# Four-token query loads with DMA transposes, bank-seeded first-layer sums and a third seven-product tile in a fused attention and MoE kernel

## The chip, the cores and the metric

One Trainium2 chip, one of its cores. Time is device microseconds (us) of one execution; the kernel before took 347.33 us, the median of three runs (346.93 to 353.17). The profile is one further execution: 350.85 us, of which 349.2 us are the span from its first to its last instruction and 1.65 us lie around it. Predicted and measured times are medians of such runs.

The engines are TensorE (PE, with its weight loads as PEld), VectorE (DVE), ScalarE (ACT), GpSimd (POOL) and SyncE (SP). Each runs its own instructions in the order of the program and waits on semaphores for the others. SP and POOL issue most DMAs; an instruction that waits on such a queue holds up everything behind it.

## What is computed

```python
B, H, S, D = 8, 8, 576, 64                       # attention, band of +-32 tokens
scores = q @ k.T / sqrt(D); masked where |i - j| > 32
attn = softmax(scores);  a = attn @ v
x = a as (4608 tokens, 512)
h = x @ w_in                                     # (512, 2048)
g = h * sigmoid(1.702 * h)
out = g @ w_out                                  # (2048, 512), float32
```

The 8 batches of 576 tokens are one row of N = 4608 tokens. A query needs only keys of its own batch that lie at most 32 tokens away.

## The kernel before

**Units and tiles.** A unit is 128 queries, shifted by 32 against the keys: unit u holds queries 128u+32 to 128u+159, as two blocks of 64, and each block meets two sets of 64 keys. Four units make a tile of 512 tokens; there are 36 units and 9 tiles. The output of a unit goes to rows 128u+32 and up.

**Attention of a unit.** `scores` runs 32 matmuls of 64 by 64 (weights are keys from `kT`, the moving operand queries from `qT`) and one exponential on ACT. `band` (DVE) multiplies with the mask. `values` runs 16 matmuls, with V from `ve` for the even block and from `vo` for the odd one; `vo` is V shifted by 64 tokens, two copies made by `odd_v`. `norm` (DVE) makes the reciprocal of the sums and writes `x` (float16, two buffers). `x_T` transposes `x` to `xT`, on PE in the head, by a DMA transpose from SP later.

**Loads of q and k.** All loads that change type are issued by POOL. `load_heads` puts four neighbouring tokens of all heads on a partition (a run of 1 KB in memory); PE transposes these (`heads_T`), and `put_T` writes them to `kT` or `qT`, with the token order restored. `load_units` puts one token on a partition (runs of 256 bytes), in one DMA for each 128 tokens, two where a batch ends inside; `units_X` then issues four DMA transposes for a tile. `kT` is a ring of 1536 tokens and `qT` one of 1024, each with a copied piece past its end (`wrap`). Before the change tiles 0 to 2 come by `load_heads` (tile 3 for keys), the rest by `load_units`. The staging tiles `ks` and `qs` have two buffers each, so a load waits until the transposes of two tiles earlier have read theirs.

**First and second layer.** In plain form a half tile (256 tokens) takes 64 matmuls of 256 columns in the first layer (`layer1`), a unit 16 matmuls of 512 columns in the second (`layer2`). A tile can instead go by seven products of quarter matrices (Winograd's form of Strassen's method): 112 matmuls of 256 columns in each layer, with sums of the operands made beforehand (`w_in_sums`, `x_sums`; `g_sums`, `w_out_sums`) and sums of the products made behind. `first_layer` has four groups; a group has seven products, named 1, 2, 6, 7, 5, 4, 3 in that order. Its two banks are A (products 1, 6, 5, 3) and E (2, 7, 4). Products 1 and 2 add up to c11: ACT copies the first one from its bank to SBUF, DVE adds the other one (L429), and ACT forms g from it. Products 6 and 7 are copied out (L442 on ACT, L446 on DVE), 5 and 4 added on DVE (L450, L454), 3 read by ACT. Each bank is filled again by the next product, so a product waits for the evacuation of the one before it in its bank. `second_layer` has 28 calls of four matmuls, on banks o and t; its last product goes out by a DVE copy (L512).

**Order.** `head` does the attention of units 0 to 6, the first layer of half tiles 0 to 2 and the second layer of units 0 to 3, all plain; `pairs` goes on in plain form; then come steps T = 3 to 10. A step does the attention of tile T, the first layer of tile T-1 and the second layer of tile T-2, in the order of the string `STEP`: S, M and V with a digit are scores, mask and values (with `norm` and `x_T`) of one of the four units; a digit and a digit is group and product of `first_layer`; c is the next call of the second layer; G, g.., o are operand sums; L issues the loads of q and k of tile T+3, l those of V; X issues the transposes of tile T+2; x has POOL make the x sums of tile T and the `vo` copies. Before the change, tiles 0 to 2 are plain and tiles 3 to 8 go by seven products; `first_layer` starts with T = 4 and `second_layer` with T = 5; d in STEP is a plain first-layer call, in T = 3 only.

Of the kernel before, what the change touches and what calls it, by code (L numbers as in the profile page):

```python
# [9 lines left out]
def _safe_warn_once(msg, *a, **kw):  # L10
# [15 lines left out]
QRING = 1024  # L26
NO = 5
STEP = ("L S0 S1 M0 M1 G c 01 c c c S2 M2 c 02 S3 M3 T d c V0 l 06 c V1 d c 07 c V2 05 c V3 X o "
        "04 c 11 c 03 d 22 c x 12 21 c 16 17 c 26 d 15 c g00 27 14 d c 25 13 c 24 c d 23 g11 c 32 c d 31 d w c c 36 37 c 35 g22 c 34 c 33 c c c")


class _Kernel:
# [50 lines left out]
    def setup(self):  # L83
# [7 lines left out]
        self.kT = cst.tile([128, 4, RING + 64], BF16, name="kT")  # L91
        self.qT = cst.tile([128, 4, QRING + 32], BF16, name="qT")
        self.k_first = cst.tile([128, 4, 64], BF16, name="k_first")
        self.q_first = cst.tile([128, 4, 32], BF16, name="q_first")
# [41 lines left out]
    def pieces(self, lo, n):  # L136

        at = lo
        while at < lo + n:
            b, s = divmod(at, self.S)  # L140
            m = min(self.S - s, lo + n - at)
            yield at - lo, b, s, m
            at += m

    def load_heads(self, i, c, heads=None):
# [6 lines left out]
        for off, b, s, m in self.pieces(512 * i, 512):  # L152
            self.nc.gpsimd.dma_start(self.stage[key][off // JT:(off + m) // JT, lo:hi, :],
                                     src[b, lo:hi, s:s + m, :].rearrange("h (p j) d -> p h (j d)", j=JT))

    def load_units(self, c, i):


        st = self.stage[c, i] = self.work.tile([128, 4, self.H, self.D], BF16, name=c + "s", tag=c + "s", bufs=2)
        src = {"q": self.q, "k": self.k}[c]  # L160
        for u in range(4):
            for off, b, s, n in self.pieces(512 * i + 128 * u, 128):
                self.nc.gpsimd.dma_start(st[off:off + n, u], src[b, :, s:s + n, :].rearrange("h s d -> s h d"))  # L163

    def units_X(self, c, i):
        dst, ring = {"q": (self.qT, QRING), "k": (self.kT, RING)}[c]
        at = (512 * i) % ring
        for u in range(4):
            self.nc.sync.dma_start_transpose(dst[:, :, at + 128 * u:at + 128 * u + 128],
                                             self.stage[c, i][:, u].rearrange("p h d -> p (h d)"))  # L170

    def wrap(self, c, i, eng):

        dst, ring, n = {"q": (self.qT, QRING, 32), "k": (self.kT, RING, 64)}[c]
        if (512 * i) % ring == 0 and i:
            self.cast(eng, dst[:, :, ring:ring + n], dst[:, :, 0:n])
# [28 lines left out]
    def put_T(self, c, i, hp, kind, eng):  # L205
        tp = self.heads_T(c, i, hp, kind)
        dst, ring = {"q": (self.qT, QRING), "k": (self.kT, RING)}[c]
        at = (512 * i) % ring
        self.cast(eng, dst[:, hp, at:at + 512].rearrange("r (p j) -> r p j", j=JT), tp.rearrange("r j p -> r p j"))
# [7 lines left out]
    def load_first(self, c, hp):  # L217
# [3 lines left out]
        self.nc.sync.dma_start(raw, src[0, 2 * hp:2 * hp + 2, 0:512, :].rearrange("h (p j) d -> p h (j d)", j=JT))  # L221
# [7 lines left out]
    def load_edge(self, c):  # L229

        self.stage[c, "edge"] = self.work.tile([64, self.H, self.D], BF16, name="edge", tag="edge")
        src = {"q": self.q, "k": self.k}[c]
        self.nc.gpsimd.dma_start(self.stage[c, "edge"], src[0, :, 512:576, :].rearrange("h s d -> s h d"))

    def edge_T(self, c, kind, eng):
        nc = self.nc
        src = self.stage[c, "edge"]
# [3 lines left out]
        if c == "k":  # L241
            self.cast(eng, self.kT[:, :, 512:576], tp)
        else:
            self.cast(eng, self.qT[:, :, 512:576], tp)

    def scores(self, u):
# [4 lines left out]
        for hp in range(4):  # L251
            for blk in range(2):
                k0 = (128 * u + 64 * blk) % RING
                q0 = (128 * u + 64 * blk + 32) % QRING
                for half in range(2):
                    lo, at = 64 * half, k0 + 64 * (half ^ blk)
                    for eo in range(2):
                        r = slice(eo * 64, eo * 64 + 64)
                        nc.tensor.matmul(sc[eo][lo:lo + 64, 2 * hp + blk, :], self.kT[r, hp, at:at + 64],  # L259
                                         self.qT[r, hp, q0:q0 + 64], start=(n == 0), stop=(n == 7))  # L260
# [39 lines left out]
    def norm(self, u):  # L300
        nc, D = self.nc, self.D
        both, acc = self.acc.pop(u)
        x = self.work.tile([128, self.H, D], F16, name="x", tag="x", bufs=2)
# [97 lines left out]
    def first_layer(self, t):  # L401
# [5 lines left out]
        def group(j):  # L407
# [19 lines left out]
            def begin(ps):  # L427
                if "c11" in st:
                    dve.tensor_add(st["c11"], ps, st["c11"])  # L429
                    return  # L430
                st["c11"] = self.work.tile([128, 2, 256], F32, name="c11", tag="s", bufs=3)
                st["c2"] = self.work.tile([128, 2, 512], F32, name="c2", tag="c2", bufs=2)
                act.copy(st["c11"], ps)  # L433

            def m1():
                begin(prod("A", q(w, 0, 0), q(xT, 0, 0), True))

            def m2():
                begin(prod("E", q(w, 1, 0), q(xT, 1, 0), True))

            def m6():
                act.copy(st["c2"][:, :, 0:256], prod("A", ws[1], xs[1]))  # L442
                gelu(q(g, 0, 0)[:, 2 * j:2 * j + 2, :], st["c11"])
# [18 lines left out]
            return {"1": m1, "2": m2, "6": m6, "7": m7, "5": m5, "4": m4, "3": m3}  # L462
# [3 lines left out]
    def second_layer(self, t):  # L466
# [5 lines left out]
        st, calls = {}, []  # L472

        def part(key, first, a, b, n):
            if first and n == 0:
                st[key] = self.bank(key, [128, 2, half], F32, "o_ps")
# [34 lines left out]
        def m3():  # L511
            dve.tensor_copy(outs(0)[:, :, half:], st["o"])  # L512
# [33 lines left out]
    def head(self):  # L546
# [12 lines left out]
        for c in "kq":  # L559
            self.load_edge(c)  # L560
# [45 lines left out]
        self.edge_T("k", "a", dve)  # L606
# [288 lines left out]
```

## Time and profile before

| | before |
|---|---|
| median of three runs | 347.33 us |
| profiled execution; its span | 350.85 us; 349.2 us |
| PE busy; DVE; ACT; POOL | 299.9; 218.5; 188.9; 158.5 us |
| mean granted TensorE clock | 0.957 |
| software DMA queue (POOL's): packets, share of 16 engines | 95504, 67.0% |
| hardware DMA queue: packets, share | 44688, 28.1% |
| first scores of `pairs` on PE | 69.08 us |
| first scores of steps 3, 4, 5, 6, 7, 8 | 104.67, 122.92, 166.21, 202.94, 236.74, 271.89 us |
| first second-layer matmuls of steps 9, 10 | 305.46, 331.49 us |

The profile gives times from the start of the span. The busy time of PE has the modelled ends of pipelined matmuls in it, so the share of PE says little; the steps are read from the starts of their first matmuls. The view of waits names, for each engine and line, what ended its idle time. The granted clock is that which the throttle left to TensorE, as a share of full speed.

### The profile page before, as it was taken

The page shows a single profiled execution, that of the slowest core. Times are in us where ns is not written, and L with a number is a line of the kernel's source. Part 1 is how long each engine was busy: PE and PEld are TensorE (multiplying, and loading weights), DVE is VectorE, ACT ScalarE, POOL GpSimd, SP SyncE. Part 2 cuts the span into 40 slices and gives each one's busy share as a digit, 9 for nine tenths or more (in the row PEclk, how much of TensorE's full clock was granted, in tenths as well). Part 3 has the DMA queues.
Part 4 walks back from the last instruction along what each step waited for, and adds up shares of the span by engine and source line. Part 5 has one row for each costly group of instructions (what it writes and reads, how often), then busy time and mean ns, then how long its engine had stood idle before and what let it go on. Part 6 is the DMA issues. An engine that isn't in the chain of part 4 may idle for free. (4 is left out here: it accounts for less than half of the span.)

```text
span 349.2 us, 9375 instructions
## 1 busy us (share of the span) xinstructions
PE 299.9 (86%) x3952; PEld 225.2 (65%) x3952; DVE 218.5 (63%) x432; ACT 188.9 (54%) x284; POOL 158.5 (45%) x206
## 2 busy tenths in 40 slices
PE   7889998999999965687788888888788889899893
PEld 4658655747575732455567676777577767788783
DVE  2841166575515382657976879687768787867832
ACT  3646355665668364244845575548364855537520
POOL 8973555157914739959926801670065005000000
PEclk9969999999999996986899999999999999999998
DMA  8999999599999998999996665566310320110113
GB/s 145 147 199 201 189 187 205 81 122 136 156 144 116 155 126 126 147 124 154 104 112 91 84 145 62 91 73 141 33 29 2 122 57 9 60 62 0 62 62 121
DMA packets 140282, 38.23 MB, mean 110 GB/s; under 512 B 124368, under 2 KB 135632, under 8 KB 140240
## 3 DMA queue, kind: packets, MB, share of 16 engines
q0 software_dynamic: 95504, 18.23, 67.0%
q1 hardware_dynamic: 44688, 19.34, 28.1%
q8 instruction: 31, 0.51, 0.6%
q10 hardware_dynamic: 48, 0.07, 0.1%
q14 instruction: 11, 0.09, 0.1%
HBM read 36.96 MB, written 9.44 MB: 133 GB/s over the span
## 5 line engine op out<-in xcount | busy, mean ns | idle before, releaser
L419 PEld LDWEIGHTS <-w_in_sb 128*128 128x128 f16 x384 | 37.5, 100 | 26.0 <-issue 14.4
L419 PE MATMUL h_ps<-xT,w_in_sb 128*128 128x256 f16 x288 | 44.4, 283 | 10.4 <-DVE c L454 6.5
L349 PE MATMUL o_ps<-w_out_sb,g 128*128 128x512 f16 x192 | 49.5, 387 | 0.0
L337 PE MATMUL h_ps<-xT,w_in_sb 128*128 128x256 f16 x384 | 48.1, 281 | 1.5 <-DMA w_in_sb<-in_moe_w_in_dram 1.5
L425 ACT ACTIVATE g<-c 128x512 f16<-128x512 f32 (+1 forms) x48 | 40.5, 845 | 14.0 <-DVE c L454 14.0
L372 POOL TENSOR_TENSOR xs<-xT 128x512 f16<-128x512 f16 x12 | 13.8, 1153 | 71.6 <-PE h_ps L419 44.1
L181 POOL DMA_DIRECT2D ve<-in_v_dram x40 | 33.9, 865 | 21.5 <-PE pv L296 14.1
L337 PEld LDWEIGHTS <-w_in_sb 128*128 128x128 f16 x384 | 37.2, 100 | 9.0 <-DMA w_in_sb<-in_moe_w_in_dram 1.8
L339 ACT ACTIVATE g<-h_ps 128x512 f16<-128x512 f32 x48 | 28.6, 597 | 26.5 <-PE h_ps L337 26.5
L479 PE MATMUL o_ps<-w_out_sb,g 128*128 128x256 f16 x288 | 40.2, 275 | 2.7 <-DVE o_sb L512 2.7
L479 PEld LDWEIGHTS <-g 128*128 128x128 f16 x384 | 36.7, 98 | 7.9 <-issue 3.0
L280 DVE TENSOR_TENSOR p<-p,mask 128x512 bf16<-128x512 bf16 (+1 forms) x48 | 28.2, 604 | 16.3 <-ACT p L264 13.1
L419 PEld LDWEIGHTS <-w_in_s 128*128 128x128 f16 x288 | 28.6, 101 | 12.2 <-issue 7.1
L419 PE MATMUL h_ps<-xs,w_in_s 128*128 128x256 f16 x192 | 29.0, 288 | 3.1 <-DVE c L429 3.1
L479 PEld LDWEIGHTS <-gs 128*128 128x128 f16 x288 | 28.2, 98 | 3.3
L433 ACT COPY c<-h_ps 128x512 f32<-128x512 f32 x24 | 14.0, 585 | 26.5 <-PE h_ps L419 26.5
L163 POOL DMA_DIRECT2D ks<-in_k_dram x22 | 18.7, 866 | 20.6 <-PE tp L201 11.6
L479 PE MATMUL o_ps<-w_out_s,gs 128*128 128x256 f16 x192 | 27.7, 273 | 0.0
L125 DVE COPY kT<-tp 128x512 bf16<-128x512 bf16 (+1 forms) x17 | 11.3, 667 | 26.1 <-PE tp L201 25.4
L264 ACT ACTIVATE p<-sc 128x1024 bf16<-128x1024 f32 x24 | 23.5, 1041 | 7.3 <-PE sc L259 7.2
L163 POOL DMA_DIRECT2D qs<-in_q_dram x27 | 22.7, 876 | 9.2 <-DMA qT<-qs 6.0
L259 PE MATMUL sc<-qT,kT 64*64 64x64 bf16 x1152 | 15.9, 197 | 12.4 <-DMA qT<-qs 7.3
(94 smaller groups left out, 527.8 us busy)
## 6 DMA issues: line engine op xcount, KB each, us to landing
out_dram<-o_sb SPq DMA_DIRECT2D x11, 512.0 KB, 2.8
ve<-in_v_dram POOLq DMA_DIRECT2D x32, 128.0 KB, 6.1
out_dram<-o_sb SPq DMA_DIRECT2D x13, 256.0 KB, 4.3
qs<-in_q_dram POOLq DMA_DIRECT2D x23, 128.0 KB, 6.3
ks<-in_k_dram POOLq DMA_DIRECT2D x20, 128.0 KB, 4.9
w_in_sb<-in_moe_w_in_dram POOLq DMA_DIRECT2D x4, 512.0 KB, 8.5
w_out_sb<-in_moe_w_out_dram POOLq DMA_DIRECT2D x4, 512.0 KB, 11.2
ve<-in_v_dram POOLq DMA_DIRECT2D x8, 64.0 KB, 6.9
```

The costliest lines, as they stand in the source:

```text
L163: self.nc.gpsimd.dma_start(st[off:off + n, u], src[b, :, s:s + n, :].rearrange("h s d -> s h d"))
L181: self.nc.gpsimd.dma_start(self.ve[m % NV][off:off + n, :, :self.D], self.v[b, :, s:s + n, :].rearrange("h s d -> s h d"))
L259: nc.tensor.matmul(sc[eo][lo:lo + 64, 2 * hp + blk, :], self.kT[r, hp, at:at + 64], self.qT[r, hp, q0:q0 + 64], start=(n == 0), stop=(n == 7))
L264: nc.scalar.activation(p.rearrange("p e b s -> p (e b s)"), both.rearrange("p e n -> p (e n)"), AF.Exp, scale=self.scale)
L280: self.nc.vector.tensor_mul(part, part, msk.to_broadcast([128, n, 2, SQ]))
L337: nc.tensor.matmul(hps[:, i, :], self.w_in_sb[:, kr, ff * 128:(ff + 1) * 128], xT[:, kr, :], start=(i == 0 and kr == 0), stop=(i == 1 and ...
L339: nc.scalar.activation(g[:, 2 * d:2 * d + 2, :], hps, AF.Gelu_apprx_sigmoid)
L349: nc.tensor.matmul(o_ps, g[:, ff, s * 128:(s + 1) * 128], self.w_out_sb[:, ff, :], start=(ff == 0), stop=(ff == self.NFF - 1))
L419: nc.tensor.matmul(ps[:, i, :], a[:, kr, (2 * j + i) * 128:(2 * j + i + 1) * 128], x[:, kr, :], start=first and i == 0 and kr == 0, stop=i ...
L425: act.activation(out, src, AF.Gelu_apprx_sigmoid)
L433: act.copy(st["c11"], ps)
L479: nc.tensor.matmul(st[key][:, p, :], a[:, kb, p * 128:p * 128 + 128], b[:, kb, :], start=first and n == 0 and kb == 0, stop=n == 3 and kb ...
```

## The change

- Queries are staged from token 32 of a tile on, so tile i holds just the queries of units 4i to 4i+3; no ring, no wrap, no edge piece. From tile 3 on they come by `load_heads` (two DMAs a tile); POOL copies the tile to an order with one token of four behind another (`spread`, 128 x 2048 elements, in the other buffer of `qs`), and `queries_X` transposes it by four DMAs. `qT` is kept as (pair of heads, tile parity, token of four, partition), and `scores` reads it with a step of 256 bytes from one query to the next.
- Keys of tile 3 come one token to a partition too, by DMA transposes. The key ring has no piece past its end; addresses wrap.
- Groups 2 and 3 of `first_layer`, and group 0 from tile 3 on, are seeded: ACT copies product 1 into bank E, product 2 accumulates there, and a new step `a` has ACT form g from the bank.
- Tile 2 goes by seven products: `first_layer` starts with T = 3, `second_layer` with T = 4. `pairs` has one block where it had two, with units 7 to 11, second layer of units 4 and 5 and first layer of half tile 3; all the sums of w_in and (on DVE) the x sums of tile 2 stand at its end, the sums of w_out one step earlier than before.
- In x of STEP the `vo` copies go before the x sums, and `spread` of tile T+3 behind them.
- `x` has four buffers; the banks of `second_layer` change names from tile to tile; its last copy goes to ACT.

```diff
-STEP = ("L S0 S1 M0 M1 G c 01 c c c S2 M2 c 02 S3 M3 T d c V0 l 06 c V1 d c 07 c V2 05 c V3 X o "
-        "04 c 11 c 03 d 22 c x 12 21 c 16 17 c 26 d 15 c g00 27 14 d c 25 13 c 24 c d 23 g11 c 32 c d 31 d w c c 36 37 c 35 g22 c 34 c 33 c c c")
+STEP = ("L S0 S1 M0 M1 G c 01 c c c S2 M2 c 02 S3 M3 T c c V0 0a l 06 c V1 c 07 c V2 05 c V3 X o "
+        "04 c 11 c 03 x 12 1a c 21 16 c 22 2a 17 c 26 15 c g00 27 14 c 25 13 c 24 c 23 c g11 31 c c 32 3a c 36 c 37 35 c g22 34 c 33 c c")
...
-        for off, b, s, m in self.pieces(512 * i, 512):
+        for off, b, s, m in self.pieces(512 * i + (32 if c == "q" else 0), 512):
...
+    def spread(self, i, eng):
+        src = self.stage["q", i].rearrange("p h (j d) -> p j h d", j=JT)
+        st = self.stage["q", i] = self.work.tile([128, JT, self.H, self.D], BF16, name="qr", tag="qs", bufs=2)
+        self.cast(eng, st, src)
+
+    def queries_X(self, i):
+        for j in range(JT):
+            self.nc.sync.dma_start_transpose(self.qT[:, :, i % 2, j, :],
+                                             self.stage["q", i][:, j].rearrange("p h d -> p (h d)"))
...
-                q0 = (128 * u + 64 * blk + 32) % QRING
+                n64 = 2 * u + blk
+                p0 = 16 * (n64 % 8)
+                qT = self.qT[:, hp, n64 // 8 % 2, :, p0:p0 + 16].rearrange("r j p -> r p j")
...
-        x = self.work.tile([128, self.H, D], F16, name="x", tag="x", bufs=2)
+        x = self.work.tile([128, self.H, D], F16, name="x", tag="x", bufs=4)
...
+            seeded = j in (2, 3) or j == 0 and t > 2
+            def m1():
+                ps = prod("A", q(w, 0, 0), q(xT, 0, 0), True)
+                st["c2"] = self.work.tile([128, 2, 512], F32, name="c2", tag="c2", bufs=2)
+                if seeded:
+                    st["c11"] = st["E"].rearrange("p (i n) -> p i n", i=2)
+                else:
+                    st["c11"] = self.work.tile([128, 2, 256], F32, name="c11", tag="s", bufs=3)
+                act.copy(st["c11"], ps)
+            def m2():
+                ps = prod("E", q(w, 1, 0), q(xT, 1, 0), not seeded)
+                if not seeded:
                     dve.tensor_add(st["c11"], ps, st["c11"])
+            def ma():
+                gelu(q(g, 0, 0)[:, 2 * j:2 * j + 2, :], st["c11"])
...
+        tag = {"o": "ot"[t % 2], "t": "to"[t % 2]}
...
-            dve.tensor_copy(outs(0)[:, :, half:], st["o"])
+            act.copy(outs(0)[:, :, half:], st["o"])
...
+        self.keys_X(3)
+        self.queries_X(3)
         for m in (14, 15, 16):
             self.load_v(m)
+        self.spread(4, pool)
         for m in (12, 13, 14):
+            self.odd_v(m, pool)
+        self.load_keys(5)
+        self.load_heads(5, "q")
         run(l2, 2)
         for m in (10, 11):
             self.odd_v(m, dve)
+        self.scores(10)
+        run(l1, 3)
+        self.scores(11)
+        self.band(10)
+        run(l1, 2)
+        self.band(11)
+        run(l1, 1)
+        self.values(10)
+        run(l1, 1)
+        self.values(11)
+        run(l1, 1)
+        self.norm(10)
+        self.x_T(10)
+        self.norm(11)
+        self.x_T(11)
+        self.odd_v(15, pool)
+        self.keys_X(4)
+        self.queries_X(4)
+        self.spread(5, pool)
+        for call in sums:
+            call()
+        self.x_sums(2)
...
-        groups = self.first_layer(T - 1) if 4 <= T <= tiles else None
+        groups = self.first_layer(T - 1) if T <= tiles else None
+        second = self.second_layer(T - 2) if T > 3 else self.plain_second((6, 7), (dve, act), "ot")
...
             elif x == "x":
-                self.x_sums(T, pool)
                 for m in range(4 * T + 4, min(4 * T + 8, self.NU)):
                     self.odd_v(m, pool)
+                self.x_sums(T, pool)
+                if T + 3 < tiles:
+                    self.spread(T + 3, pool)
```

## The prediction

> **What bounds the kernel now.** I read first the busy times by stretch, cut at the first scores of `pairs` and of steps 3 to 7 on PE.
>
> ```profile
> core 0: us, PE busy (x) PEld busy (x) DVE busy (x) ACT busy (x) POOL busy (x), PEclk, DMA share, GB/s
> 69.08:104.67 35.59, 34.50 (x469) 22.57 (x469) 18.04 (x48) 22.55 (x36) 21.89 (x29) 1.00 1.48 136
> 104.67:122.92 18.25, 17.84 (x288) 11.62 (x287) 7.86 (x17) 11.09 (x15) 10.51 (x12) 1.00 1.53 136
> 122.92:166.21 43.29, 29.68 (x338) 18.68 (x338) 26.34 (x42) 19.03 (x27) 32.56 (x40) 0.80 1.69 134
> 166.21:202.94 36.73, 30.39 (x418) 24.64 (x418) 30.22 (x54) 21.38 (x31) 23.43 (x28) 0.95 1.17 108
> 202.94:236.80 33.86, 29.25 (x423) 24.23 (x426) 26.85 (x47) 20.66 (x30) 13.57 (x16) 1.00 0.58 85
> ```
>
> Step 4 (third stretch) takes 43.29 us for fewer matmuls than step 6 runs in 33.86, PE idle for 13.6 of them and its clock at 0.80. Steps 5 and 6 have PE and DVE both near 27 to 30 us. Next the waits of the whole run:
>
> ```profile
> engine line waited for: us in total, times, longest us
> ...
> DVE x L309 <- DMA xT<-x: 11.4, 8, 2.7
> ...
> POOL ks L163 <- DMA kT<-ks: 9.0, 1, 9.0
> ...
> PE sc L259 <- DMA qT<-qs: 7.3, 1, 7.3
> ...
> PE o_ps L479 <- DVE o_sb L512: 2.7, 5, 0.9
> ```
>
> The 7.3 us are step 4's: unit 19 needs the transposes of tile 5, which stand late on SP, as its order of time shows:
>
> ```profile
> 118.11 2.97 SPq L322 DMA_TRANSPOSE xT<-x  x2
> 121.16 8.00 SPq L169 DMA_TRANSPOSE kT<-ks  x4
> 129.27 5.45 SPq L169 DMA_TRANSPOSE qT<-qs  x4
> ```
>
> Step 3 was 18.25 us short, so its own transposes ran into step 4. Last the chain that ended last, in a regular step:
>
> ```profile
> 211.27 0.60 DVE p L280
> 212.02 0.70 DVE x L309
> 212.86 2.41 DMA xT<-x
> 215.42 0.55 issue
> 215.97 0.68 DVE c L450
> 216.80 0.69 DVE x L309
> 217.49 0.61 DVE c L454
> ```
>
> It is DVE's for most of the attention, with the `x` buffers between. In that step DVE stands still only 0.50 us for them, since other DVE work fills the rest of the 2.41; in step 7 it is 2.5, in step 5 1.88.
>
> **PE.** In a run of 32, a 256-column matmul costs 0.109 us ((3.66-0.27)/31, L337), and in a run of 16 a 512-column one 0.216 ((3.63-0.39)/15, L349). Tile 2 plain is 128 x 0.109 + 64 x 0.216 = 27.8 us, by products 224 x 0.109 = 24.4: 3.4 less. Keys of tile 3 take 32 transposes off PE (four runs of 0.41, 1.6 us) and four DVE copies of 0.69. They add four DMA transposes on SP, at 1.3 us each, ahead of the query ones.
>
> **Pairs and steps 3 and 4.** Up to the start of the plain first layer (79.44) nothing changes. Then come eight calls of 0.87, two scores and two values of 0.45: 88.2. Unit 11 now waits for the first key transpose of tile 3. SP is free at 81.0 (the `x` pair before it), so 82.3 plus some 2 us to land (xT and kT rows: 2.4 to 3.7 from issue) is 84.5, where PE comes at 82.5: +2. Unit 12 waits for all four query transposes, since each holds one token of four of every unit; before, one was enough. Eight at 1.33 (four took 5.33) end at 91.6, landed near 94.5; PE comes at 91. So step 3 starts near 94.5, against 104.67 with one half tile and two units of the second layer more behind it.
>
> Step 3 has 112 x 0.109 + 32 x 0.216 + 8 x 0.45 = 22.7 us of PE; step 6 has 24.4 + 3.6 = 28.0 and takes 33.86, so 5.9 over. I give step 3 the same: 28.6, ending at 123. The sums of w_in (eight of 0.6) and the x sums of tile 2 (four of 0.43) now stand before its first mask on DVE, about 6.5 us behind the last plain matmul; PE has 5.6 us of scores and layers ahead of the first values, so this costs at most 2 and lies beside the wait for queries. The sums of w_out (four of 1.22) come a step earlier; steps 4 and 5 lose what steps 3 and 4 get.
>
> Step 4's stall of 7.3 goes: with step 3 at 28 us its transposes end before. What is late next is POOL. `spread` is one copy of 2048 elements: at the rate of the `vo` copies (528 in 0.62 us) 2.4 us, at that of the x sums (512 in 1.15) 4.6; I take 2.4, being a copy too. For tile 4 it can't write before the transposes of tile 3 have read its buffer (94.5). Behind it on POOL are six `vo` copies (0.68 each, 101), five key and two query issues (0.87 and 0.72, 106.5), unit 15's `vo`, and the next `spread`, which needs that query load landed: the 128 KB rows show 4.9 to 6.3 us, the 448 KB row 14.8, so 112 to 120, say 115. Then step 3's own loads (117.5 to 125.5), `vo` (until 134) and only then, as the order is changed, the x sums of tile 3 (134 to 139). Product 06 of step 4 wants these at 130. So 0 to 9 us of new wait; I take 5. Step 4 then takes 31 + 5 and ends at 159, where step 5 started at 166.21: gain 7. Ends: 151 if POOL keeps up and step 3 starts at 91; 168 if both waits are full and the clock falls to 0.80 again as after the old stall.
>
> **Steps 5 to 8** (36.73, 33.86, 35.15 and 33.57 us from the starts of their first matmuls). DVE loses three c11 additions (start to start 0.60) and the last o_sb copy (0.60): 2.4 us, most of it in stretches that the chain gives to DVE. ACT gets the copy (0.58) and has 20.66 of 33.86 busy; its copy of product 1 becomes a wait for PE in front of product 2, where the order leaves two to four calls of 0.44. The wait for `x` gives 1.88, 0.5, 2.5 and about 0.5; after it SP's issue is late next (1.5 us a transpose against 1.5 us a unit), which holds nobody on DVE. Step 5 also loses w_out sums (2.4) and its low clock (0.95 x 36.73 is 34.9). Taking two thirds of the DVE time as on the path: 31.5, 31.5, 31.5 and 31 where there were 139.3: gain 13.8. The lower end is a third, 9; the upper all, 17. Steps 9 and 10 wait 0.93 us each for the o_sb copy at their start; with banks changing names this goes: 1.8, of which I take 1.5.
>
> **What it may cost.** No row shows a matmul that reads its moving operand in steps. A score matmul adds 0.008 us to a run ((0.71-0.45)/32), four side by side. The nearest rows are copies reading the same 256-byte steps from a bank: DVE 0.692 against 0.686 straight, ACT 0.585 against 0.583, so nothing. The far end is four that no longer lie side by side, 0.033 each, +0.8 us a unit, 29 us over 36 units. Shorter than now it can't be, as the columns are the same. I take 0.1 a unit, near the copies, 24 units from step 3 on, half beside ACT's exponentials: 1.2 us. The Trainium skill, "SBUF — State Buffer", section on Door 1, says that engines read at full rate only where consecutive reads share a 16-byte line, which speaks against this change; it gives no price, and no row here shows it.
>
> `spread` also meets DVE. A gs sum of 512 elements takes 0.425 us in the median and 1.275 beside POOL's copies of 0.62. Six `spread`s are between 0 (beside PSUM work) and 2.4 each; I take 0.8 each, as in that row, 4.8 in all, 3.5 on the path. The same page, section on the two sides of SBUF, calls the port that DVE and POOL share an exclusive lock for the whole instruction, which would make it up to 2.4 each, 14; the row shows a wait of about one POOL copy. On POOL's issue side 27 query loads of 0.876 become 12 of about 0.72, 15 us less, for 14.4 of `spread` and five key issues for two (+2.9). Fewer and larger query packets ease the software queue (67.0% of the engines), whose transfers no step after 5 waits for; I price that at nothing, within the end of 151 above.
>
> **Sum.** 7 + 13.8 + 1.5 - 1.2 - 3.5 = 17.6 from the span of 349.2; the profile has 1.65 more around it and stands 3.5 over the median of 347.33, so the median comes to 329.7, taken as 330.
>
> **Rivals.** (1) All of the DVE time counts and POOL keeps up: 15 + 17 + 1.8 - 1.2 - 1 = 31.6, 316 us. For it: step 3 has a third more time for transposes; against: the query buffer holds POOL until 94.5. (2) The queues take back the first gain: SP and POOL late in steps 3 and 4, step 5 at 168, clock low: -2 + 9 + 1.5 - 1.2 - 3.5, 3.8 us, 343.5. The 9.0 and 7.3 us waits above show how such a queue acts. (3) The other side: the strided read serializes the scores. 29 us over 36 units take away all: 347.33 - 18.8 (the sum without its 1.2) + 29 = 357.5. It decides from about 0.5 us a unit, where the gain is gone; the copy rows speak against it. (4) The change doesn't save what it says: a seeded product 2 waits for ACT as long as DVE was spared, since the start of a step has ACT busy with 5 us of exponentials (first seed at 207.5 of 204.4 to 210.5); that is the lower end of 9, 335.
>
> **Chances.** Forecast, 323 to 337, 0.55 (with rival 4); rival 1, below 323, 0.15; rival 2, 337 to 347, 0.19; rival 3 and what is slower still, 0.11. The range 316 to 344 leaves out 0.11 of (3), 0.04 of (2) and about 0.05 of (1). A change of under about 2% can't be told from none here (340.4 to 354.3): faster 0.55 + 0.15 + 0.09 = 0.79; within 0.10 + 0.02; slower 0.09.
>
> **What would show it.** First scores of step 3 near 94.5 and of step 5 near 159, scores no longer ending a wait of 7 us for qT; POOL's x sums of tile 3 ending before or after product 06 of step 4; steps 6 to 8 near 31.5; a run of 32 score matmuls at 0.45 still; gs sums above 1.3 us where a `spread` lies beside them; L309 without waits for xT. Wrong it would be if the starts of step 3 or 5 are late by more than 5 us, or score runs go above 0.9 us.

## The result and the profile after

The changed kernel takes 364.77 us in the median (363.3 to 367.59), the kernel before 349.64 in the runs beside it: a ratio of 1.0469, interval 1.0333 to 1.0606. It is slower by 15 us, where 17 us less were forecast. The ratios leave out disturbed runs, so they can differ from the quotient of two medians by up to 0.01; a hundredth is 3.5 us.

The busy times by stretch of the changed kernel (columns as before), cut at the first scores of steps 3, 4, 6 and 7:

```profile
103.88:138.21 34.33, 29.12 (x337) 19.40 (x336) 26.71 (x47) 18.60 (x26) 22.76 (x26) 0.95 1.65 131
138.21:180.77 42.56, 34.68 (x417) 27.96 (x416) 27.41 (x46) 21.45 (x31) 24.15 (x29) 0.88 1.30 100
216.03:252.80 36.77, 32.70 (x417) 26.57 (x416) 28.12 (x43) 21.48 (x32) 27.32 (x30) 1.00 1.09 131
252.80:286.73 33.93, 32.40 (x418) 26.71 (x418) 22.91 (x43) 21.48 (x32) 8.70 (x10) 1.00 0.20 48
```

Step 3 starts at 103.88, not at 94.5, and step 5 at 180.77, not at 159. Steps 6 and 7 last 36.77 and 33.93, where the kernel before had 33.80 and 35.15. PE is busy for 32.4 us of a regular step instead of 29.2, though it runs the same number of matmuls. The costliest groups say which: first the scores of the changed kernel, then those of its variant that reads the queries straight (run `a1_straight_read` below).

```profile
L259 PE MATMUL sc<-qT,kT 64*64 64x64 bf16 x1152 | 44.4, 317 | 2.6 <-ACT p L264 1.9
```
```profile
L259 PE MATMUL sc<-qT,kT 64*64 64x64 bf16 x1152 | 16.5, 202 | 15.3 <-ACT p L264 11.7 <-DMA kT<-ks 2.6 <-ACT g L339 0.7
```

The same 1152 matmuls hold PE for 44.4 us instead of 15.9 before. In the second row PE's wait for the exponentials `p` is 11.7 us instead of 1.9: part of what the slow scores take, PE would otherwise have waited. Of the waits of the changed kernel, those that matter are

```profile
POOL qr L123 <- DMA qT<-qr: 25.1, 2, 15.8
...
PE h_ps L419 <- POOL xs L372: 7.0, 1, 7.0
```

The 7.3 us for `qT` and the 11.4 us of `x` for `xT` are gone from the list. In their place PE waits 7.0 us in step 4 for POOL's x sums, which GpSimd's order of time shows behind the odd values (`vo`), and these behind a wait of 8.05 us for V:

```profile
144.42 0.68 POOL L189 COPY vo<-ve 64x528 bf16<-64x528 bf16 x1 [8.05 <-DMA ve<-in_v_dram]
...
151.20 1.14 POOL L372 TENSOR_TENSOR xs<-xT 128x512 f16<-128x512 f16 x1
```

### The profile page after: what moved, and what is told of

Its sections match the earlier page's. It is cut to its first block, busy times and chain, and to the rows that moved or that the text cites. A ratio compares the mean times of both kernels' runs of the same rounds, so it can differ in the third digit from the quotient of the medians.

```text
span 364.2 us, 9362 instructions
## 1 busy us (share of the span) xinstructions
PE 324.5 (89%) x3948; PEld 250.2 (69%) x3948; DVE 221.8 (61%) x427; ACT 200.0 (55%) x296; POOL 162.8 (45%) x199
## 4 chain that ended last, share of the span: by engine, by line
PE 49%; DVE 18%; ACT 13%; DMA 9%; issue 6%; POOL 4%; DVEq 0%; POOLq 0%; ACTq 0%
PE h_ps L419 15%; PE o_ps L484 13%; PE h_ps L337 6%; PE sc L259 6%; ACT g L425 5%; PE o_ps L349 5%; DMA ve<-in_v_dram 4%; DVE p L280 3%; DVE gs L372 3%; DVE c L454 2%; DVE c L450 2%; DMA qs<-in_q_dram 2%; PE pv L296 2%; DMA out_dram<-o_sb 2%; DVE g L372 2%
## 5 line engine op out<-in xcount | busy, mean ns | idle before, releaser
L419 PEld LDWEIGHTS <-w_in_sb 128*128 128x128 f16 x448 | 42.6, 98 | 23.0 <-issue 14.5
L419 PE MATMUL h_ps<-xT,w_in_sb 128*128 128x256 f16 x336 | 51.2, 275 | 7.0 <-ACT h_ps L436 4.8
L425 ACT ACTIVATE g<-h_ps 128x512 f16<-128x512 f32 x48 | 28.6, 595 | 45.1 <-PE h_ps L419 37.9
L259 PE MATMUL sc<-qT,kT 64*64 64x64 bf16 x1152 | 44.4, 317 | 2.6 <-ACT p L264 1.9
L259 PEld LDWEIGHTS <-kT 64*64 64x64 bf16 x1152 | 36.4, 129 | 8.8 <-issue 7.6
L425 ACT ACTIVATE g<-c 128x1024 f16<-128x1024 f32 (+1 forms) x36 | 33.9, 962 | 9.7 <-DVE c L458 9.7
L337 PE MATMUL h_ps<-xT,w_in_sb 128*128 128x256 f16 x256 | 34.3, 291 | 2.9 <-ACT g L339 2.9
L450 DVE COPY c<-h_ps 128x512 f32<-128x512 f32 x28 | 19.3, 688 | 26.2 <-PE h_ps L419 26.2
L189 POOL COPY vo<-ve 64x528 bf16<-64x528 bf16 x26 | 18.5, 713 | 36.1 <-DMA ve<-in_v_dram 35.1
L349 PE MATMUL o_ps<-w_out_sb,g 128*128 128x512 f16 x128 | 32.4, 380 | 0.0
L337 PEld LDWEIGHTS <-w_in_sb 128*128 128x128 f16 x256 | 25.5, 104 | 8.5 <-issue 3.7
L495 ACT COPY kept<-o_ps 128x512 f32<-128x512 f32 x21 | 12.4, 589 | 31.7 <-PE o_ps L484 31.7
L123 POOL COPY qr<-qs 128x2048 bf16<-128x2048 bf16 x6 | 12.0, 2006 | 39.2 <-DMA qT<-qr 25.1
```

The costliest lines, as they stand in the source:

```text
L189: eng.tensor_copy(vo[0:64], nxt)
L337: nc.tensor.matmul(hps[:, i, :], self.w_in_sb[:, kr, ff * 128:(ff + 1) * 128], xT[:, kr, :], start=(i == 0 and kr == 0), stop=(i == 1 and ...
L349: nc.tensor.matmul(o_ps, g[:, ff, s * 128:(s + 1) * 128], self.w_out_sb[:, ff, :], start=(ff == 0), stop=(ff == self.NFF - 1))
L419: nc.tensor.matmul(ps[:, i, :], a[:, kr, (2 * j + i) * 128:(2 * j + i + 1) * 128], x[:, kr, :], start=first and i == 0 and kr == 0, stop=i ...
L425: act.activation(out, src, AF.Gelu_apprx_sigmoid)
L450: dve.tensor_copy(st["c2"][:, :, 256:512], prod("E", ws[2], xs[2], True))
```

## The experiments

The first theory after the result: the strided read costs 29 us of PE and hid the forecast gain. The second: the gain isn't there even without it, and late queues, table loads and operand sums are the main loss.

**Straight read.** A score matmul reads 64 consecutive columns of `qT` (other queries meet the keys); all else as changed.

```
-qT = self.qT[:, hp, n64 // 8 % 2, :, p0:p0 + 16].rearrange("r j p -> r p j")
+qT = self.qT[:, hp, n64 // 8 % 2].rearrange("r j p -> r (j p)")[:, 4 * p0:4 * p0 + 64]
```


> The changed kernel, but each score matmul reads 64 neighbouring elements of the query tile where it read 16 times 4 with a step of 256 bytes; queries then meet other keys, so the output is another one, with the same number and shape of instructions. Theory 1 (the step in the read is the main loss): a run of 32 score matmuls goes from 1.27 us back to 0.45, and the time falls by 36 units x 0.82 = 29.5 us less some 4 that lie beside the exponentials: 338 to 344 us, below the kernel before. Theory 2 (rival: the POOL queue, the added table loads in the first block and the late operand sums are the main loss, the longer score runs being mostly hidden by the exponentials): the runs get short all the same, but the time stays above 352 us. Both: the wait of 7 us of step 4 for the x sums stays, since POOL is not touched.

354.53 us (352.87 to 357.96), ratio 1.0148 (1.0081 to 1.0215). The scores are back at 0.45 us a run of 32, and 0.0321 of the ratio, 11 us, goes with the stride. But the kernel is still slower than before, and the time lies where the second theory put it; its parts are tested below. Of 29 us of PE only 11 show. By step starts nearly all of that lies ahead of step 3: `pairs` starts at 66.40 instead of 73.98 (seven units of 0.83 are 5.8 of it) and lasts 27.61 instead of 29.90. Step 7 lasts 34.02 against 33.93 with the stride, but not at the same clock. These are its rows in this run and in the next one (runs of 16 elements, where the scores are as fast):

```profile
243.95:277.97 34.02, 30.66 (x418) 24.64 (x417) 23.05 (x43) 21.42 (x32) 8.34 (x10) 0.95 0.17 48
```
```profile
243.52:276.78 33.26, 29.39 (x417) 24.01 (x416) 23.08 (x43) 21.30 (x32) 8.97 (x10) 1.00 0.21 49
```

In steps 5 to 7 the straight read has a granted clock of 0.95, 0.91 and 0.95, the strided one 1.00 in all three. At a clock of 1.00, as in the second row, the stride costs some 0.7 us of step 7. So waits of PE and a lower clock hide it there together; why the clock differs was not tested.

**Where the price begins.** Two kernels. The changed one with runs of 16 consecutive elements:

```
+qT = self.qT[:, hp, n64 // 8 % 2, :, p0:p0 + 16]
```


> The changed kernel with the columns of a block in the order token-of-four outside, partition inside: four runs of 16 neighbouring elements (32 bytes) where there were 64 single ones; the columns then stand in another order than the mask, so the output is another one. Theory 1a (the price is for every element that lies in another 16-byte line than the one before): 0.45 to 0.50 us for a run of 32 score matmuls, the price of 64 jumps being 0.82 and of 4 jumps a sixteenth, 0.05. Rival 1b (any pattern of more than one dimension costs, or the tile's distance of 256 bytes does): above 0.8 us.

The kernel before with another length of run from unit to unit:

```
+qv = self.qT[r, hp, q0:q0 + 64]
+run = (16, 8, 4, 2, 1, 1)[u % 6] if u >= 12 else 16
+if run < 16:
+    qv = qv.rearrange("r (a b e) -> r b a e", a=4, e=run)
...
```


> The kernel before, where the score matmuls of units 12 to 35 read their 64 queries in a permuted order: units 0 mod 6 straight, 1 mod 6 in runs of 8 elements (16 bytes), then of 4, 2, 1 and 1, each run 32 bytes or more away from the one before; the rest is untouched, but the output is another one. A price by itself: theory 1a: 0.45 us for straight and for runs of 8, more the shorter the run, and near 1.25 us for single elements; if the price is per jump to another line, 8, 16, 32 and 64 jumps give 0.55, 0.65, 0.85 and 1.27. Rival 1b: all permuted ones alike, near 1.27. Theory 2 has nothing to say of it, but if single elements cost less than 0.7 us, the step of 256 bytes or something else of the change is the cause and not the order.

With runs of 16 a score matmul takes 193 ns in the median, as straight (355.14 us, one run). PE's order of time in the second kernel (355.05 us, one run); the units are 24 and 25 in one row, 26, 27, then 28 and 29 in one row, 30, and last 32 and 33 in one row:

```profile
208.18 0.71 PE L263 MATMUL sc<-qT,kT 64*64 64x64 bf16 x64
212.01 0.45 PE L263 MATMUL sc<-qT,kT 64*64 64x64 bf16 x32 [0.48 <-ACT p L268]
213.37 0.65 PE L263 MATMUL sc<-qT,kT 64*64 64x64 bf16 x32
241.79 2.04 PE L263 MATMUL sc<-qT,kT 64*64 64x64 bf16 x64
246.05 0.45 PE L263 MATMUL sc<-qT,kT 64*64 64x64 bf16 x32
...
276.07 0.93 PE L263 MATMUL sc<-qT,kT 64*64 64x64 bf16 x64
```

Straight and runs of 8 together take 0.71, as two straight units do; runs of 4 take 0.45, runs of 2 take 0.65 (runs of 4 and of 2 together 0.93, 0.22 over 0.71), and two units of single elements 2.04. The granted clock is 1.00 in all these stretches; a straight unit, too, takes 0.64 where the clock is 0.50, as in the row of 239.54 further below. So at steps of 32 bytes a jump every 8 bytes is free, one every 4 bytes costs 0.2 us a unit, and one at every element some 0.65; in the changed kernel, whose steps are 256 bytes, it is 0.83. A price for each jump, 0.55, 0.65, 0.85 and 1.27 as expected for the four patterns, it isn't.

**One-token queries.** The changed kernel with queries loaded one token to a partition, as the keys are: no spread, straight read.

```
+self.nc.gpsimd.dma_start(st[off:off + n, u], self.q[b, :, s:s + n, :].rearrange("h s d -> s h d"))
...
-self.load_heads(3, "q")
+self.load_queries(3)
-self.spread(3, pool)
...
+qT = self.qT[:, hp, q0:q0 + 64]
```


> The changed kernel with queries loaded and transposed one token to a partition as before (still from token 32 of a tile on, in a ring of 1024), so without the copy on POOL and with a straight read; all else of the change stays. Theory 1: scores 0.45 us a unit; POOL's order loses two waits for query transposes, so the wait of step 4 for the x sums shrinks from 7.0 us to 0 to 3, and step 3 starts by some us earlier: 332 to 340 us, below the straight read alone by 3 to 8. Theory 2: 345 to 352, since the queues that it blames are still as they are in the kernel before or worse (27 to 30 query loads of 0.88 us on POOL).

> The changed kernel with one-token queries once more, unaltered, beside the next three. Theory A (the seeds and ScalarE's copy cost what the two single edits gained): 347 to 351 us as before, so that all of the 6.4 and 3.8 us belongs to the edits. Theory B (the granted clock of 0.95 in that profile's regular steps was the chip's and not the kernel's): 342 to 345 us, and a profile with the clock at 1.00 in steps 6 and 7.

348.89 us, ratio 0.9997 (0.9959 to 1.0035), and 347.42, 0.9963 (0.9925 to 1.0), in another set of runs: the time of before, though third tile, seeds and four x buffers are in it, and 9 us above the range of the first theory. Four-token loads, their transposes and the spreads cost 0.015 to 0.019, 5 to 6.5 us. One part of that can be seen in the changed kernel, where a sum of second-layer operands on VectorE lies beside a spread; alone such a sum takes 0.42 us:

```profile
224.69 2.09 POOL L123 COPY qr<-qs 128x2048 bf16<-128x2048 bf16 x1
225.06 2.00 DVE L372 TENSOR_TENSOR g<-g 128x512 f16<-128x512 f16 x1
```

The repetition lies in theory A's range and not in B's, and its granted clock in steps 6 and 7 is 0.95 again: the two gains told of below aren't a matter of one chip.

**Single parts in the kernel before.** Four x buffers alone (two edge tiles of the head use them too, for room), and seeds alone.

```
...
-x = self.work.tile([128, self.H, D], F16, name="x", tag="x", bufs=2)
+x = self.work.tile([128, self.H, D], F16, name="x", tag="x", bufs=4)
```


> The kernel before with four x buffers and nothing else of the change (the two edge tiles of the head borrow x slots, for room). VectorE's waits for xT<-x (11.4 us in all, 5.4 of them in steps 5 to 8) go in either theory. Theory 1, the prediction's: VectorE's time in the steps is on the path, so most of it shows, 343 to 346 us. Theory 2 (a step's second half is full on TensorE and its first half is a chain through ScalarE's exponentials and gelus, so time freed on VectorE lies beside other work): 347 to 350 us.

341.74 us, ratio 0.9796 (0.9744 to 0.9848): 7 us, the first theory's side and a little more than it asked for. Steps 5 to 7 give 3.5 us, of the 4.9 that the prediction read as waits there; step 4 gives 5.2 (38.09 for 43.29), its clock at 0.87 for 0.80.

```
+ps = prod("A", q(w, 0, 0), q(xT, 0, 0), True)
...
+    st["c11"] = st["E"].rearrange("p (i n) -> p i n", i=2)
...
+act.copy(st["c11"], ps)
...
+ps = prod("E", q(w, 1, 0), q(xT, 1, 0), not seeded)
...
```


> The kernel before with seeded first-layer sums in groups 0, 2 and 3 of tiles 3 to 8 and nothing else of the change; the first two products of groups 2 and 3 change places, as in the change. Three additions of 0.69 us a step leave VectorE in six steps. Theory 1 (two thirds of it on the path): 1.2 to 1.4 us a step, 341 to 344 us. Theory 2 (hidden under TensorE's full second half; ScalarE's copy becomes a wait in front of product 2): 348 to 352 us.

360.39 us, 1.0304 (1.0238 to 1.037): both theories missed, by 8 us and more. Its waits name a cost that neither had: PE's h_ps for ACT's g, 20.5 us in 29 waits. Product 7 writes the seeded bank E anew, and in the order of before the gelu that reads it is issued only after product 6. The change issues that gelu earlier (step "a"), and with it this wait is 2.2 us; so this run prices seeds in the old order, not the change's.

**The two edits on ScalarE, one by one,** in the kernel with one-token queries: the last second-layer copy back on VectorE, and no seeds.

```
-act.copy(outs(0)[:, :, half:], st["o"])
+dve.tensor_copy(outs(0)[:, :, half:], st["o"])
```


> The changed kernel with one-token queries (348.89 us), the last second-layer copy of each tile back on VectorE. Theory 1 (VectorE's time is what counts, ScalarE's copy is free): 0.4 us a step slower, 350 to 352 us. Theory 2 (the copy on ScalarE stands straight in front of the next step's exponentials, which the second pair of scores waits for): 0.5 us a step faster, 344 to 347 us, and TensorE's wait of its scores for ScalarE's p falls from 1.7 to about 1.1 us in a regular step.


```
-seeded = j in (2, 3) or j == 0 and t > 2
+seeded = False
```


> The changed kernel with one-token queries (348.89 us), no group seeded: copy into SBUF and addition on VectorE as before the change, in the new order. Theory 1 (an addition saved is two thirds on the path): 2.7 saved additions of 0.69 us a step come back, 7 steps, 354 to 358 us. Theory 2 (they are hidden): 347 to 350 us, and the waits of h_ps for ScalarE's copy h_ps (3.1 us in steps 5 to 8) go.

342.48 us (0.9821, 0.9764 to 0.9878), and 345.1 us in the median (339.77 to 346.53, too wide for a ratio). Each undoes an edit that was to spare VectorE, and each is faster, by 1.5 and 2 us more than theory 2's range. PE's wait for the exponentials at the second pair of scores in step 7 falls from 1.74 us to 1.26 and 1.47. But now PE waits in step 4 for the x sums (5.9 and 4.3 us), which the kernel with both did not. So the next runs separate GpSimd's lateness from the edits. First both undone, then the x sums ahead of the odd values, then also the scores of units 10 and 11 together:

> One-token queries, no group seeded, and the last second-layer copy back on VectorE. Theory A: both gains stand beside each other, 338 to 341 us, regular steps near 31.5 to 32. Theory B: both were the same chip's clock, 342 to 345 us, regular steps near 32.6.


```
+self.x_sums(T, pool)
 for m in range(4 * T + 4, min(4 * T + 8, self.NU)):
     self.odd_v(m, pool)
-self.x_sums(T, pool)
```


> The kernel of the run before with the x sums ahead of the odd values on GpSimd, as they stood before the change. Theory A (GpSimd's lateness in step 4 is a wait that counts, 4.3 to 5.9 us for the x sums): 3 to 5 us below the run before and no wait of h_ps for xs. Rival (the odd values, now behind the sums, or the keys' transposes are late next): within 1.5 us of the run before, with a wait for vo or kT of 3 us or more in its place.


```
 self.scores(10)
-run(l1, 3)
 self.scores(11)
+self.gelu_table()
 self.band(10)
```


> The kernel of the run before with the scores of units 10 and 11 side by side in front of the first layer of tile 3, so that ScalarE's table changes twice there and not four times (1.28 us each). Theory A (the table loads stand on TensorE's path, 3.6 to 5.0 us of waits of h_ps for g): 2 to 4 us below the run before. Rival (step 3 waits for its transposes anyway): within 1 us, the wait of its first scores for kT or qT longer by what was saved.

Both undone: 342.52 us in the median (337.36 to 344.2), ratio 0.9716 (0.965 to 0.9783), too wide to tell the theories apart. With the x sums first: 336.26 us, 0.962 (0.957 to 0.967), no wait for xs, as theory A had it. Scores together: 336.03, 0.9596 (0.9555 to 0.9636), the same. There the rival was right: two of ScalarE's six table loads in `pairs` go (the kernel before has four there), and with them PE's waits of h_ps for g, 4.3 us, but the scores wait 6.3 us for `kT` where they waited 2.5.

**Seeds and copy, four cases with the x sums first.**

> One-token queries, x sums first, copy on VectorE, groups seeded as in the change: beside the 336.3 us without seeds. Theory S (a seed makes ScalarE's copy a wait in front of product 2, worth more than the addition it saves): 339 to 341 us. Rival (the single edit gained by GpSimd's timing in step 4, and seeds are neutral): 335 to 338 us.

> One-token queries, x sums first, no seeds, last second-layer copy on ScalarE: beside the 336.3 us with it on VectorE. Theory S (the copy stands in front of the table load and the exponentials of the next step, 0.58 us a step and a little more): 339 to 341 us. Rival (neutral): 335 to 338 us.

> One-token queries and x sums first, seeds and the copy on ScalarE both as in the change. Theory S with both prices adding up: 342 to 345 us. Rival (late GpSimd and late exponentials hid one another in step 4, where this kernel showed no wait for xs): 346 to 349 us, no change against the 347.4 and 348.9 us with the x sums last. Second rival (only the x sums mattered): 336 to 339 us.

| x sums first, one-token queries | last copy on VectorE | on ScalarE |
|---|---|---|
| no seeds | 336.26 us, 0.962 | 340.83 us, 0.9772 (0.9724 to 0.982) |
| seeds | 341.3 us, 0.9777 (0.9725 to 0.983) | 343.73 us, 0.9835 (0.9782 to 0.9888) |

Two lie in the range of theory S, seeds alone 0.3 us above it: alone the seeds cost 5.0 us and the copy 4.6, together 7.5. The first case comes from the set of runs before the other three; by the ratios, each against the kernel before beside it, it is 5.5, 5.3 and 7.5 us. With both edits the x sums first gain 4 to 5 us against 348.89 and 347.42, though PE showed no wait for xs there; its second pair of scores in step 5 waited 3.60 us for the exponentials, now 1.74.

**The x sums first in the changed kernel itself.**

> The changed kernel itself with only the x sums put ahead of the odd values and the spread on GpSimd. Theory S (its wait of 7.0 us for xs in step 4 counts): 357 to 360 us instead of 364.8. Rival (the odd values or the queries' transposes come as much later, so that the wait changes its name): 362 to 366 us, with 4 us or more of TensorE's wait for vo, kT or qT in its place.

359.72 us, 1.0322 (1.0263 to 1.0382): 5 us less, as theory S had it; step 4 lasts 37.88 instead of 42.56, and its PE waits for no xs.

## Why the prediction was wrong

Three steps failed: the price of the strided read, the path that VectorE's time was taken to lie on in steps 5 to 8, and the lengths of steps 3 and 4.

Held against the forecast's own step starts, the changed kernel's trace is 9.4 us late at the start of step 3 (103.88 for 94.5), loses 5.7 in step 3 (34.33 for 28.6), 6.6 in step 4 (42.56 for 36), 11.5 in steps 5 to 7 (105.96 for 94.5) and 4.2 from the start of step 8 on (77.5 for 73.2). Less the 4.7 that the forecast took for stride and spread apart from the steps, that is the 32.6 us between the forecast span of 331.6 and the measured 364.2.

By the runs the stride made the forecast too low by 10 us, VectorE's time by 14, the lengths of steps 3 and 4 by 8. The spread was too small by 2, and the runs beside it have the kernel before 2 us higher than the median that the sum stood on; the x buffers gave 1.6 more than priced. From 329.7 that makes 364.1, where 364.77 was measured. So near a hit is partly luck, because these parts overlap: the x buffers, for one, gave most of their 7 us in step 4, whose length is counted by itself.

**The strided read.** The step was "The nearest rows are copies reading the same 256-byte steps from a bank ... so nothing" and "I take 0.1 a unit". It is 0.83 a unit, the far end that the prediction had named (0.8, 29 us): rival 3's price at its full size. That four matmuls no longer lie side by side, as rival 3 had it, isn't shown; prices of 0.2 and 0.65 for other patterns say that it isn't a matter of all or nothing. The copies read a bank of PSUM on DVE and ACT; no row showed PE reading its moving operand from SBUF in single elements, and nearness of the step length was taken for nearness of the engine and the memory. And one of the rows says something else. The 0.692 us of DVE's copies of `kT` (16-bit elements) was set beside 0.686 of a copy of float32; a straight copy of as many 16-bit elements from a bank, `xT`, takes 0.422 in the same profile before:

```profile
L125 DVE COPY kT<-tp 128x512 bf16<-128x512 bf16 x16 | 11.0, 691 | 26.1 <-PE tp L201 25.4 <-PE tp L198 0.7
L125 DVE COPY xT<-tp 128x512 f16<-128x512 f16 x4 | 1.7, 422 | 1.8 <-PE tp L326 1.8
```

So DVE took 0.27 us longer for the steps, and only ACT took as long for both (0.585). Rival 3 was wrong in its turn that all 29 us would be on the path. This is the start of step 7 in the kernel of the first case of the table (no seeds, copy on VectorE), from the wait of the second pair of scores on (its first pair starts at 225.65):

```profile
229.65 0.45 PE L259 MATMUL sc<-qT,kT 64*64 64x64 bf16 x32 [1.00 <-ACT p L264]
230.02 0.61 PE L484 MATMUL o_ps<-w_out_sb,g 128*128 128x256 f16 x4
230.47 0.60 PE L419 MATMUL h_ps<-xT,w_in_sb 128*128 128x256 f16 x4
```

Even here PE waits 1.00 us for the exponentials of the first pair. In the changed kernel the first pair takes 2.31 us and not 0.71, and the wait at the same place is 0.20: the stride fills it. From the first pair to the second it is 4.80 us there and 4.74 with the straight read. Ahead of step 3 the stride shows, as the step starts say. The prediction's start of step 3, 94.5, is met by the straight read (94.01); the other 9.9 us are the stride's.

**VectorE's time in steps 5 to 8.** The step was "Taking two thirds of the DVE time as on the path: 31.5, 31.5, 31.5 and 31 ... gain 13.8", with ACT's copy at nothing because ACT "has 20.66 of 33.86 busy". Its part for the `x` buffers had the right sign: 3.5 of 4.9 us in steps 5 to 7, and 5.2 in step 4, where none was priced. Its part for seeds and copy (2.4 us in each of four steps, two thirds of it, 6.4) has the wrong sign: 7.5 us lost over the kernel. (The prediction names only the 13.8; 6.4, 5.4 for the waits for `x` and 1.8 for the clock of step 5 make 13.6.) VectorE did get the time. Step 7 without either edit, from the kernel above, then steps 6 and 7 with both, from the last case of the table:

```profile
225.65:257.94 32.29, 29.15 (x418) 24.05 (x417) 26.72 (x47) 20.63 (x31) 10.09 (x12) 1.00 0.33 60
```
```profile
199.12:232.54 33.42, 29.39 (x418) 24.00 (x418) 23.94 (x43) 21.31 (x32) 13.49 (x16) 1.00 0.61 97
232.54:267.39 34.85, 30.70 (x418) 24.69 (x418) 24.24 (x43) 21.41 (x32) 9.91 (x12) 0.95 0.29 56
```

DVE falls from 26.72 to 23.94 and 24.24 us, and the steps take 33.42 and 34.85 instead of 32.29. Single steps scatter: in the three kernels with neither edit steps 6 and 7 take 32.29 to 33.65, 32.7 in the mean.

Part of the loss comes with the clock. In the three profiles with one-token queries and both edits the granted clock is 0.95 in five of the steps 6 and 7 and 1.00 in one; in the seven profiles with one edit or none it is 1.00 in thirteen of fourteen. With both edits the step at 1.00 takes 33.42, those at 0.95 take 34.05 to 34.85. In the last row the clock is 0.68 from 237.7 to 243.0, behind the waits shown below, and 1.00 elsewhere. Step 6 has the same first wait, 1.74 us, and keeps 1.00, so what brings the clock down stays open.

PE has 29.15 of 32.29 us busy without the edits. It stands idle 1.0 us at the step's start, waiting for ScalarE, and 1.7 between 247 and 252, where it waits 1.30 for VectorE's copy of product 7. There VectorE is busy 4.90 of 5.00 us, and with both edits 4.96 of 5.00 in a like stretch of step 6 (221 to 226, where PE waits 0.90 for that copy): what the edits took off VectorE lay elsewhere. What they added lay at the step's start. Here is ScalarE at the start of step 7 of the kernel with one-token queries and both edits:

```profile
239.78 0.57 ACT L517 COPY o_sb<-o_ps 128x512 f32<-128x512 f32 x1
240.36 1.28 ACT L264 ACT_TABLE_LOAD   x1
241.66 1.94 ACT L264 ACTIVATE p<-sc 128x1024 bf16<-128x1024 f32 x2
```

The copy stands straight in front of the table load (ScalarE changes from gelu to exponentials) and the exponentials. And in step 7 of the kernel with both edits and the x sums first (its first scores at 232.54):

```profile
237.27 0.45 PE L259 MATMUL sc<-qT,kT 64*64 64x64 bf16 x32 [1.74 <-ACT p L264]
237.65 0.61 PE L484 MATMUL o_ps<-w_out_sb,g 128*128 128x256 f16 x4
238.68 0.93 PE L419 MATMUL h_ps<-xT,w_in_sb 128*128 128x256 f16 x4 [0.42 <-ACT h_ps L436]
239.54 0.64 PE L259 MATMUL sc<-qT,kT 64*64 64x64 bf16 x32
```

From the first to the second pair of scores it is 4.73 us here and in step 8; in the other three cases of the table 4.00 without the two edits, 4.27 with seeds alone, 4.48 with the copy alone. At this place the prices add up: 0.27 and 0.48 a step. (In steps 5 and 6 the four cases scatter more, 4.27 to 5.08.) The seed's copy then holds PE 0.42 in front of product 2, where the row of 230.47 without seeds has no wait, and the additions on VectorE held PE 0.2 us in that whole run; over the run PE waits for these copies 5.8 us in 12 places (seeds alone), against 2.4 for ScalarE's other copies without seeds. The share of busy time on ScalarE was the wrong reading: 61% of the step, but at the start of step 7 with one-token queries it has work without a gap above 0.3 us from 0.8 to 11 us. Rival 4 named the place and stopped at a gain of a third. The starts of steps 7 and 8 (2 x 0.73) and the longer waits (5.8 - 2.4) make 4.9 of the 7.5 us; the rest wasn't followed to its end, and the lower clock bears on it.

**Steps 3 and 4.** The steps were "I give step 3 the same: 28.6" and "Step 4 then takes 31 + 5", of which the 5 held. In the best case, which has no wait for the x sums, step 3 starts at 92.84, earlier than forecast, and the two last 32.45 and 34.88 us: 7.7 over 28.6 and 31. The clock there is 0.89 and 0.95, which alone makes some 4 us of 22.7 and 28.0 us of PE work (an estimate: 22.7/0.89 and 28.0/0.95), and the scores wait 2.5 us for `kT`. The 5.9 us that were carried over from step 6 came from a step at 1.00.

**Point by point.** *Tile 2 by products and the new order of `pairs`:* against the kernel before with four x buffers (0.9796), the best case has 0.962, 6 us, all other parts of the change that no run takes singly among them. The two table loads added there were overlooked, and cost nothing, since the transposes are late next (scores together). *GpSimd in step 4:* "0 to 9 us of new wait; I take 5" was right in mechanism and place: 7.0 us in the trace, 5 us in the time. The size is partly luck: the sums begin at 151.2 and not at 134, and PE comes for them at 147.9 and not at 130. *The wait for `x`:* gone, as said. *Spread:* 3.5 taken beside VectorE; with its loads it is 5 to 6.5. *Steps 9 and 10:* 1.5 was to be won by the bank names, and PE's waits of o_ps for o_sb did go from 2.7 us to 0.6. But from the start of step 8 to the end the changed kernel takes 77.5 us, before 77.3. With the copy on VectorE it is 74.9 to 75.2, with copy and seeds and fast scores 76.6 to 78.1: a gain was there, and the two edits took it back. *What was to show it:* operand sums above 1.3 us beside a spread were right (2.00), and the signs of a wrong forecast, score runs above 0.9 us and a late step 3, both came.

The parts, by ratios of separate runs, each taken from the run next to it: four x buffers -0.020, third tile, order and the rest -0.018, seeds and copy +0.022, x sums late about +0.014, four-token loads and spreads +0.017, stride +0.032; 0.962 is 3.8% below the kernel before, with one-token queries, no seeds, the copy on VectorE and the x sums first; the scores together (0.9596) are not told apart from it.

## What to carry to other kernels

Price an access pattern by a row in which the same engine reads elements of the same size from the same memory, and where there is none, take the far end into the forecast, or measure the pattern in a kernel of its own before building on it. Work moved from a busy engine to an idle one is priced by when it runs there: what stands in front of the chain that opens each step costs most of its time (0.48 of 0.57 us here), whatever the engine's share. And where PE already fills nine tenths of a step, time saved on another engine counts only in the stretch where PE waits for that engine.

## What the runs showed of the hardware

PE reads a moving operand of 64 bf16 columns at full rate from runs of 4 elements (8 bytes) up; runs of 2 make 32 score matmuls 0.65 us instead of 0.45, single elements 1.0 to 1.2 at steps of 32 bytes and 1.3 at steps of 256. The Trainium skill, "SBUF — State Buffer", section on Door 1, has at least two reads of a 16-byte line absorb the access. Here two elements of a line were not quite enough (0.65 us), and four were (0.45), though each run of four lay in another line than the one before.

A VectorE sum of 512 elements that lies beside a GpSimd copy of 2048 took 2.00 us instead of 0.42, about as long as the copy (2.09).
